# Half transposes, plain odd scores and two late sums in a sigmoid-attention and two-MLP kernel on one core

## The chip, the cores and the metric

The kernel runs on one core of a Trainium2 chip. The metric is the device time of one execution in microseconds; the figure compared is the median of several executions. The core's engines are TensorE (PE, with its weight loads shown apart as PEld), VectorE (DVE), ScalarE (ACT), GpSimd (POOL) and SyncE (SP), and 16 DMA engines move data between HBM and the core's memories.

## What is computed

Sigmoid attention over 4 batches, 12 heads, 448 positions and 64 dimensions, and then two MLP layers over the 1792 tokens it gives (768 wide, 2048 hidden). In short:

```python
scores = scale * q @ k.T - log(S)            # q, k, v: (4, 12, 448, 64) float32
attn = sigmoid(scores) @ v
x = attn moved to (1792, 768)
h = x @ w_in;  x = elu(h) @ w_out            # first layer: (1792x768)(768x2048), (1792x2048)(2048x768)
h = x @ w2_in; out = (h - tanh(h)) @ w2_out  # second layer, the same sizes
```

## The kernel before

**Numbers on PE.** PE multiplies fp32 operands in two forms. In plain fp32 one matmul is exact enough by itself. In fp32r a number is split into a head (its value copied to fp32r) and a rest (value minus head); a product is then three matmuls, head x head, head x rest and rest x head, added in PSUM. The scores and both MLP layers are made the second way, the values and the last rows of the scores in plain fp32.

**Attention** (`attention`, 16.70 to 143.80 us and its ends) works on 24 pairs of heads, two pairs to a round: an even pair n and an odd one, n + 1. Keys are taken as 384 positions in three groups of 128 (`u` = 0, 1, 2) and a rest of 64, queries as 448. The two heads of a pair lie on the two halves of the array's rows, so that the scores' matmuls come in twos. In a round PE runs, in this order: `scores` of the even pair (18 matmuls, L401); `transpose` of the next even and the next odd pair (eight and seven blocks by an identity, L332 keys, L334 the keys' rests, L336 queries); `scores` of the odd pair; `pv_rest` (L439, the rests' values); `scores_rest` (L412, the rests' scores of the next round); `pv` (L428, the values of both pairs, with the sigmoids of the even and then the odd pair). Between them, ACT and DVE drain the transposes from PSUM to `plain` (`drain`, L357 and L359) and split each pair into head and rest in `es` (`hi`, L372 and L374; `lo`, L382), and ACT makes each group of scores into weights by a sigmoid (`sig`, L422; `sig_rest`, L418). ACT and DVE also narrow the MLP weights that come in as eight-byte numbers (`load` and what it calls, L632, L635, L639), and split parts of x for the first layer (L803, L809).

**What sets the order.** Each step is an `op` with the engine's queue, a cost, the steps it waits for, and a due time from `PHASES` (with `CYCLE`, `SHIFTS`, `FIRST_PAIRS`); `Sched` simulates the engines and writes the instructions of each engine in the order that comes out. On the chip an engine runs its own list in that order and waits at each step for what the step needs. The scores, the odd transposes and the rest share three double banks of PSUM (`ring`), taken in turn; the even transposes take the values' banks (`t_flat`). A bank is free when the sigmoid, or the drain, that reads it is done.

**The MLP layers** each make their two products by a scheme of seven smaller products (P1 to P7, named in `PROD` and `W_OF`) from sums of blocks of the two operands. For the first layer's `w_out` the needed forms of the weights are made during attention, block by block: `p_sum` makes S1, S2, S3 and S4 on DVE (L692), `p_store` writes seven forms to HBM (`p_forms`) in three stores. The first layer's second product then runs from 357.3 to 560.6 us in two slices of tokens, 512 and 384 wide (`s` = 0, 1; L992), product after product; each product takes its weights in four chunks `d` of 384 KB: `ow_load` on SP's queue into one of three places in `first` (later two in `spare`), `ow_head` on ACT (L953), `ow_rest` on DVE (L957), into one of four places (places of P1, P5 and P6 are kept for the second slice). The other operand comes in half chunks `j` by `og_load`, `og_head` (L964) and `og_rest` (L968) through landing places named by the ring "g0", ten of them: seven and the temporaries 23 to 25, which lie in `second`. P3 uses S4, P7 uses S3, P6 uses S2. When a product is through, `o2_out` steps add it to the others on ACT and DVE.

## Time and profile before

| | us |
|---|---|
| median of 3 runs | 974.3 (974.08 to 976.07) |
| the profiled execution | 973.46 |
| its span in the trace | 971.7 |
| attention, up to PE's first MLP matmul | 153.94 |
| first layer's first product | 154 to 357.3 |
| first layer's second product | 357.3 to 560.6 |
| second layer | 560.6 to the end |

The span is the time between the first and the last instruction of the trace; the execution's own time holds 1.76 us more. In the timelines each row is a run of like instructions on one engine: when the first began, from there to the end of the last, engine, line, what it reads and writes, and how many. Where an engine stood idle ahead of a row, the idle time and what ended it stand in brackets at its end. PE's rows overlap, since its matmuls are pipelined: the start of a row is when the one before it has made way.

### The profile page before, as it was taken

What the parts mean: (1) busy time and instruction counts of PE and PEld (TensorE: products, weight loads), DVE (VectorE), ACT (ScalarE), POOL (GpSimd) and SP (SyncE); (2) the same over time, 40 slices, a digit from 0 to 9 for tenths busy, and PEclk for the clock granted to TensorE, in tenths of its full rate; (3) what the DMA queues carried; (4) which work ended last, traced back from release to release, by engine and by line L of the source; (5) the groups of instructions that cost most, each with busy time, mean ns of one, the idle gap of its engine ahead of it and who ended that gap; (6) DMA issues with size and microseconds to landing.
All of it is one profiled execution on the core that took longest, in us unless ns stands there. A gap on an engine that the chain in (4) does not pass through costs nothing.

```text
span 971.7 us, 15458 instructions
## 1 busy us (share of the span) xinstructions
PE 964.0 (99%) x5306; PEld 835.2 (86%) x5306; DVE 763.4 (79%) x1118; ACT 606.6 (62%) x953; POOL 101.0 (10%) x102
## 2 busy tenths in 40 slices
PE   9999999999999999999999999999999999999998
PEld 5555556889999998888999988888889999999998
DVE  4889998988888777688896988787777788666673
ACT  6889889666666675656665664444444565446652
POOL 2223311001111100000000200111111000000000
PEclk9999999999999999999999999999999999999999
DMA  8999971465555599999966416555554984545442
GB/s 250 301 348 337 331 250 38 140 224 198 188 189 181 189 303 392 412 410 398 366 223 218 139 55 244 195 191 193 187 182 169 355 288 145 145 150 180 130 145 84
DMA packets 145151, 220.18 MB, mean 227 GB/s; under 512 B 21488, under 2 KB 102960, under 8 KB 144816
## 3 DMA queue, kind: packets, MB, share of 16 engines
q1 hardware_dynamic: 143168, 218.64, 66.0%
q8 instruction: 41, 0.67, 0.3%
q10 hardware_dynamic: 1904, 0.56, 0.2%
q14 instruction: 38, 0.31, 0.1%
HBM read 143.39 MB, written 75.76 MB: 226 GB/s over the span
## 4 chain that ended last, share of the span: by engine, by line
PE 96%; DVE 1%; DMA 1%; ACT 1%; issue 0%; SPq 0%; DVEq 0%; ACTq 0%
PE psa L837 13%; PE psd L837 12%; PE psx L837 10%; PE psv L992 7%; PE psu L992 7%; PE psw L992 7%; PE psa L992 6%; PE psb L992 6%; PE psb L837 6%; PE pv L428 5%; PE sps L401 5%; PE psy L992 5%; PE psx L992 3%; PE psd L992 1%; PE pv L439 1%; PE sps L412 1%
## 5 line engine op out<-in xcount | busy, mean ns | idle before, releaser
L964 ACT ACTIVATE XB<-t 128x384 fp32r<-128x384 f32 (+1 forms) x111 | 62.0, 563 | 29.5 <-PE psw L992 8.4
L422 ACT ACTIVATE an<-sps,bias 128x896 f32<-128x896 f32 x72 | 70.5, 1020 | 12.1 <-PE sps L401 11.8
L968 DVE TENSOR_TENSOR XB<-t,XB 128x384 fp32r<-128x384 f32 (+1 forms) x111 | 68.3, 625 | 4.6 <-ACT XB L964 4.5
L752 POOL TENSOR_TENSOR second<-second 128x384 f32<-128x384 f32 x13 | 14.6, 1120 | 546.0 <-DMA spare<-p_forms 209.9
L428 PE MATMUL pv<-an,vl 128*64 128x448 f32 x288 | 56.8, 543 | 0.0
L837 PE MATMUL psa<-XB,W 128*128 128x512 f32 x192 | 54.2, 391 | 0.0
L401 PE MATMUL sps<-e 64*128 64x448 f32 x432 | 52.8, 380 | 0.6 <-ACT plain L357 0.4
L964 ACT ACTIVATE XB<-spare 128x512 fp32r<-128x512 f32 (+1 forms) x72 | 40.8, 571 | 19.0 <-DMA spare<-x_forms 5.5
L401 PEld LDWEIGHTS sps<-e 64*128 64x128 f32 x432 | 37.5, 184 | 16.7 <-issue 8.0
L428 PEld LDWEIGHTS pv<-an,vl 128*64 128x64 f32 x288 | 19.6, 137 | 36.3 <-issue 31.7
L968 DVE TENSOR_TENSOR XB<-spare,XB 128x512 fp32r<-128x512 f32 (+1 forms) x72 | 44.0, 621 | 8.4 <-ACT XB L964 8.4
L254 POOL COPY first<-raw_qk 128x384 f32<-128x384 f32 (+1 forms) x44 | 37.6, 877 | 90.2 <-DMA raw_qk<-in_k_dram 45.6
L992 PE MATMUL psu<-XB,XB 128*128 128x384 f32 (+1 forms) x192 | 46.2, 348 | 0.0
L992 PE MATMUL psv<-XB,XB 128*128 128x384 f32 (+1 forms) x192 | 46.2, 348 | 0.0
L992 PE MATMUL psw<-XB,XB 128*128 128x384 f32 (+1 forms) x192 | 46.2, 348 | 0.0
L837 PEld LDWEIGHTS psa<-XB,W 128*128 128x128 f32 x192 | 36.0, 188 | 7.5
L870 ACT ACTIVATE spare<-spare 128x512 f32<-128x512 f32 (+1 forms) x64 | 36.7, 576 | 1.4
L992 PE MATMUL psa<-XB,XB 128*128 128x384 f32 (+1 forms) x156 | 36.9, 347 | 0.0
L992 PE MATMUL psb<-XB,XB 128*128 128x384 f32 (+1 forms) x156 | 36.9, 347 | 0.0
L992 PEld LDWEIGHTS psu<-XB,XB 128*128 128x128 f32 x192 | 34.7, 188 | 1.9
L992 PEld LDWEIGHTS psv<-XB,XB 128*128 128x128 f32 x192 | 34.7, 188 | 1.9
L992 PEld LDWEIGHTS psw<-XB,XB 128*128 128x128 f32 x192 | 34.7, 188 | 1.9
(372 smaller groups left out, 2703.5 us busy)
## 6 DMA issues: line engine op xcount, KB each, us to landing
x_forms<-R1b SPq DMA_DIRECT2D x58, 256.0 KB, 2.0
first<-p_forms SPq DMA_DIRECT2D x36, 384.0 KB, 6.8
t<-x_forms SPq DMA_DIRECT2D x64, 192.0 KB, 3.1
t<-x_forms SPq DMA_DIRECT2D x47, 256.0 KB, 5.0
x_forms<-t SPq DMA_DIRECT2D x46, 256.0 KB, 2.0
x_forms<-R1b SPq DMA_DIRECT2D x58, 192.0 KB, 3.0
first<-in_moe_w_in_dram SPq DMA_DIRECT2D x13, 768.0 KB, 5.7
second<-in_moe_w_in_dram SPq DMA_DIRECT2D x13, 768.0 KB, 6.2
```

The lines of the kernel that those rows point to most:

```text
L254: nc.gpsimd.tensor_copy(out=(ql, kl)[w][:, n % NL].rearrange("p c (h d) -> p c h d", h=2), in_=x)
L401: nc.tensor.matmul(out=ps[:, j, :S], lhsT=e[lanes, EW * kz + u * 128:EW * kz + (u + 1) * 128], rhs=e[lanes, EW * qz + KW:EW * qz + EW], st ...
L412: nc.tensor.matmul(out=ps[c:c + 64, j, :S], lhsT=plain[0][lanes, RS * x:RS * x + RS], rhs=kq(x)[lanes, KW:], start=True, stop=True,)
L422: nc.scalar.activation(out=a, in_=T.pop(("s", n, u))[:, :, :S], func=ACTF.Sigmoid, bias=bias, scale=scale)
L428: nc.tensor.matmul(out=T["o", n][D * j:D * j + D, :S], lhsT=vl[m % NVL][:, x, 3 * j + u], rhs=a[:, j], start=False, stop=(u == 2), skip_gr ...
L439: nc.tensor.matmul(out=T["o", n][D * j:D * j + D, :S], lhsT=vrest[n // NR % 2][lanes, m % (NR // 2), j], rhs=a[lanes, j], start=True, stop ...
L752: by.tensor_tensor(out=out, in0=x, in1=y, op=op)
L837: nc.tensor.matmul(out=ps, lhsT=w[wz][:, k0:k0 + 128], rhs=xs[xz][:, kk], start=(opens and n == 0), stop=(n == 3 * KH - 1), skip_group_che ...
L870: nc.scalar.activation(out=r, in_=r, func=ACTF.Exp, scale=-1.0)
L964: nc.scalar.activation(out=at_place(og_place[i, s, p, j], 0, i)[:, :HW[s]], in_=T["graw", i, s, p, j], func=ACTF.Copy)
L968: nc.vector.tensor_tensor(out=lo, in0=T.pop(("graw", i, s, p, j)), in1=f(hi), op=ALU.subtract)
L992: nc.tensor.matmul(out=T["o2", tag], lhsT=lhsT, rhs=rhs, start=(p in OPENS and j == 0 and x == 0), stop=(j == NG - 1 and x == 2), skip_gro ...
```

## The change

The change has three parts, and the due times of attention (`CYCLE` 5800 for 6000, `PHASES`) are set anew with them.

1. *Transposes in halves.* From pair 4 on (`OWN`), a block of 128 x 128 is transposed as two halves, one on the upper 64 rows of the array and one on the lower 64, into two PSUM banks: 16 matmuls for the even pair, 14 for the odd one. The blocks come out 128 columns wide, so that queries are kept with 16 columns of padding to each 112 (`queries`), cleared once. The drains become two copies, one for each half of `plain`.
2. *Scores.* Only even pairs from the second on are split (`split`), head and rest both on DVE. Odd pairs and the first pair multiply in plain fp32: 6 matmuls where 18 were. There is a third tile of `plain` for it.
3. *The first layer's second product.* `p_sum` makes S1 and S2 only, and `p_forms` holds five forms. S4 = A12 - S2 and S3 = A22 - S2 are made when they are needed: `ow_load` brings A12 or A22, and once for both S2 (into `second`), and `ow_sum` subtracts on DVE. P3 and P7 run side by side: chunk 0 of P3, chunk 0 of P7, chunk 1 of P3, and so on (`o_bits`). "g0" has seven landing places.

```diff
-CYCLE = 6000
+CYCLE = 5800
+OWN = 4
@@ attention
-            krest = [ld_p.tile([128, 2, DD], F32, name=f"krest{i}") for i in range(2)]
+            krest = [first[:, NL * (R + 3) * DD + 2 * DD * i:][:, :2 * DD].rearrange("p (m x) -> p m x", m=2) for i in range(2)]
+            def split(n):
+                return n % 2 == 0 and n > 0
+            def plain_of(n):
+                return plain[1 + n // 2 % 2 if n % 2 else 0]
             def side_by_side(n, w):
+                if w == 0 and OWN <= n < OWN + NL:
+                    nc.gpsimd.memset(ql[96:, n % NL], 0.0)
             def transpose(n):
+                if n >= OWN:
+                    for i in range(len(blocks(n))):
+                        turn(n, i)
+                    return
+            def blocks(n):
+                return ([] if n % 2 else [krest[n // NR % 2][:, n // 2 % 2]]) + [kl[:, n % NL, c] for c in range(3)] + [ql[:, n % NL, c] for c in range(R)]
+            def turn(n, i):
+                ps, x = t_flat(n), blocks(n)[i]
+                for z in range(2):
+                    lanes = slice(64 * z, 64 * z + 64)
+                    nc.tensor.transpose(ps[z][:, 64 * i:64 * i + 64], x[lanes], ident[lanes, lanes])
             def drain(n, x):
+                if n >= OWN:
+                    m = len(blocks(n))
+                    out = plain_of(n).rearrange("p (i x) -> p i x", x=128)[:, :m, 64 * x:64 * x + 64]
+                    in_ = t_flat(n)[x].rearrange("p (i x) -> p i x", x=64)[:, :m]
             def hi(n):
-                if hi_on(n) == "ACT":
-                    nc.scalar.activation(out=es[n % 2][:, :EW], in_=kq(n), func=ACTF.Copy)
-                else:
-                    nc.vector.tensor_copy(out=es[n % 2][:, :EW], in_=kq(n))
+                nc.vector.tensor_copy(out=e[:, :EW], in_=kq(n)[:, :EW])
             def scores(n, u):
-                for x, (kz, qz) in enumerate(((0, 0), (0, 1), (1, 0))):
+                for x, (kz, qz) in enumerate(((0, 0), (0, 1), (1, 0)) if split(n) else ((0, 0),)):
                     for j in range(2):
                         lanes = slice(64 * j, 64 * j + 64)
+                        ks, qs = (e[lanes, EL * z:EL * z + EL] if split(n) else kq(n)[lanes, :EL] for z in (kz, qz))
                         nc.tensor.matmul(
-                            out=ps[:, j, :S], lhsT=e[lanes, EW * kz + u * 128:EW * kz + (u + 1) * 128], rhs=e[lanes, EW * qz + KW:EW * qz + EW],
+                            out=by_chunk(ps[:, j, :S]), lhsT=ks[:, u * 128:(u + 1) * 128], rhs=queries(qs[:, KW:]),
@@ weights of the first layer's second product
             def p_store(j, c):
-                part, at, a0, a1 = ((2, 0, 0, 1), (3, 0, 1, 3), (3, 2, 3, 7))[c]
+                part, at, a0, a1 = ((2, 0, 0, 1), (3, 0, 1, 3), (3, 2, 3, 5))[c]
+            def o_bits(s):
+                firsts, lasts = o_order(0, s)[:3], o_order(0, s)[5:]
+                bits = [(p, d) for p in firsts for d in range(NG // 2)]
+                bits += [(p, d) for d in range(NG // 2) for p in ("P3", "P7")]
+                return bits + [(p, d) for p in lasts for d in range(NG // 2)]
+            OF_TWO = {"P3": "A12", "P7": "A22"}
+            def ow_load(i, s, p, d, x):
+                t = ow_raw(i, s, p, d) if x == 0 else ow_other(i, s, p, d)
+                form = OF_TWO.get(p, W_OF[p]) if x == 0 else "S2"
+                nc.sync.dma_start(out=t.rearrange("p (j e) -> p j e", j=2), in_=p_forms()[:, FORMS.index(form), 2 * d:2 * d + 2])
+            def ow_other(i, s, p, d):
+                return second[:, d % 2 * CW:(d % 2 + 1) * CW]
+            def ow_sum(i, s, p, d):
+                t = ow_raw(i, s, p, d)
+                nc.vector.tensor_tensor(out=t, in0=t, in1=ow_other(i, s, p, d), op=ALU.subtract)
-                RINGS["g0"] = tuple(old) + (5, 6) + tuple(sorted((t for t in held if t not in old), key=held.get)) + (23, 24, 25)
+                RINGS["g0"] = tuple(old) + (5, 6) + tuple(sorted((t for t in held if t not in old), key=held.get))
-                for x in W_SUMS:
+                for x in ("S1", "S2"):
                     op("p_sum", (j, x), "DVE", dve(DH), p_sum, both + stored + ...)
```

How the instructions stand on the engines, before and after. A row is a line, an operation, what it writes and reads, the size, and how many of it follow each other; a number behind a name tells apart tiles that follow each other in one place.

On PE, one round in the middle of attention, before: `pv_488` and `pv_489` hold the even pair's transposes, `sps` the odd pair's and the scores; `e_83` is the even pair's split, `e_123` the odd pair's.

```order
L401 MATMUL sps<-e_83 128x448 x18
L332 MATMUL pv_488<-ident,first 128x128 x3
L334 MATMUL pv_488<-ident,krest_116 128x128
L336 MATMUL pv_489<-ident,first 128x112 x4
L332 MATMUL sps<-ident,first 128x128 x3
L336 MATMUL sps<-ident,first 128x112 x4
L401 MATMUL sps<-e_123 128x448 x18
L439 MATMUL pv_545<-ar,vrest_118 64x448 x2
L439 MATMUL pv_548<-ar,vrest_118 64x448 x2
L412 MATMUL sps<-plain_121 64x448 x2
L412 MATMUL sps<-plain_122,plain_121 64x448 x2
L428 MATMUL pv_545<-an,vl_119 64x448 x6
```

A round of the kernel after, from the last of the even pair's half transposes (L367) on; `plain_121` and `plain_119`, `plain_120` are drained pairs.

```order
L367 MATMUL pv_326<-ident,first 128x64
L367 MATMUL pv_327<-ident,first 128x64
L367 MATMUL sps<-ident,first 128x64 x14
L421 MATMUL sps<-plain_121 128x448 x6
L459 MATMUL pv_383<-ar,vrest_115 64x448 x2
L459 MATMUL pv_386<-ar,vrest_115 64x448 x2
L432 MATMUL sps<-plain_119 64x448 x2
L432 MATMUL sps<-plain_120,plain_119 64x448 x2
L448 MATMUL pv_383<-an,vl_118 64x448 x6
L448 MATMUL pv_386<-an,vl_118 64x448 x6
L421 MATMUL sps<-e_83 128x448 x18
```

The order of the steps is the same; the odd pair's 18 matmuls on `e_123` have become 6 on `plain_121`, behind 14 half transposes.

On ACT, one round of attention before: from the three sigmoids of an even pair (L422) to those of the next.

```order
L422 ACTIVATE an<-sps,bias 128x896 x3
L357 ACTIVATE plain_121<-pv_625 128x512
L357 ACTIVATE plain_122<-sps 128x832
L422 ACTIVATE an<-sps,bias 128x896
L632 ACTIVATE XB_71<-XB_71 128x768
L422 ACTIVATE an<-sps,bias 128x896
L372 ACTIVATE e_83<-plain_121 128x832
L418 ACTIVATE ar<-sps,bias 128x896
L422 ACTIVATE an<-sps,bias 128x896
L632 ACTIVATE R1b<-R1a 128x768
L803 ACTIVATE XA<-R0a 128x512
```

The same on ACT after (L442 the sigmoids, L388 the drains, L651 the narrowing, L822 the copies of parts of x).

```order
L442 ACTIVATE an<-sps,bias 128x896 x3
L388 ACTIVATE plain_121<-sps 128x7x64
L388 ACTIVATE plain_119<-pv_738 128x8x64
L442 ACTIVATE an<-sps,bias 128x896
L651 ACTIVATE XB_71<-XB_71 128x768
L651 ACTIVATE XB_71<-XA_70 128x768
L442 ACTIVATE an<-sps,bias 128x896 x2
L438 ACTIVATE ar<-sps,bias 128x896
L822 ACTIVATE XA<-R0a 128x512
L651 ACTIVATE R1b<-R1a 128x768
```

The odd pair's drain has moved ahead of the even pair's, the split's copy (L372) is gone, and the two narrowing steps stand side by side behind the first sigmoid of the odd pair.

On DVE, at P3's first weights in the wide slice, before: rests of weights (L957), each behind its head on ACT, among rests of the other operand (L968) and narrowing of the second layer's weights (L635, L639).

```order
L957 TENSOR_TENSOR XB_72<-first,XB_72 128x768
L968 TENSOR_TENSOR XB_1753<-t,XB_1753 128x512
L635 TENSOR_SCALAR R1b<-R1b 128x768
L639 SCALAR_TENSOR_TENSOR R1b<-R1b 128x768
L968 TENSOR_TENSOR XB_1753<-spare,XB_1753 128x512
L957 TENSOR_TENSOR XB_72<-first,XB_72 128x768
L968 TENSOR_TENSOR XB_1753<-t,XB_1753 128x512
L635 TENSOR_SCALAR R1a<-R1a 128x768
L639 SCALAR_TENSOR_TENSOR R1a<-R1a 128x768
L968 TENSOR_TENSOR XB_1753<-t,XB_1753 128x512
L957 TENSOR_TENSOR e_83<-first,e_83 128x768
```

The same place after (L993 the rests of weights, L986 the new sums, L1004 the other operand's rests, L654 and L658 the narrowing).

```order
L986 TENSOR_TENSOR first<-first,second 128x768
L1004 TENSOR_TENSOR XB_1711<-t,XB_1711 128x512
L658 SCALAR_TENSOR_TENSOR R1a<-R1a 128x768
L1004 TENSOR_TENSOR XB_1711<-t,XB_1711 128x512
L654 TENSOR_SCALAR R1b<-R1b 128x768
L993 TENSOR_TENSOR XB_72<-first,XB_72 128x768
L1004 TENSOR_TENSOR XB_1711<-spare,XB_1711 128x512
L658 SCALAR_TENSOR_TENSOR R1b<-R1b 128x768
L986 TENSOR_TENSOR first<-first,second 128x768
L1004 TENSOR_TENSOR XB_1711<-spare,XB_1711 128x512
L986 TENSOR_TENSOR first<-first,second 128x768
L993 TENSOR_TENSOR XB_72<-first,XB_72 128x768
```

A sum stands ahead of each rest, several steps before it, and two of the sums follow each other with one step between.

## Rows read from the trace of the kernel before

**Rows 1.** Part 1 of the page: busy time, share of the span, instructions, by engine.

```profile
PE 964.0 (99%) x5306; PEld 835.2 (86%) x5306; DVE 763.4 (79%) x1118; ACT 606.6 (62%) x953; POOL 101.0 (10%) x102
```

**Rows 2.** Table of stretches: length, busy by engine, granted clock, DMA share, GB/s.

```profile
16.70:143.80 127.10, 126.72 (x938) 69.95 (x934) 112.57 (x166) 109.18 (x135) 33.29 (x38) 1.00 0.98 318
407.90:440.50 32.60, 32.60 (x145) 27.02 (x144) 26.11 (x38) 20.91 (x33) 0.00 (x0) 1.00 1.04 412
```

**Rows 3.** PE's timeline of one round: start, us, instruction, count, idle before and releaser.

```profile
95.24 2.09 PE L401 MATMUL sps<-e 64*128 64x448 f32 x18
97.26 0.55 PE L332 MATMUL pv<-ident,first 128*128 128x128 f32 x3
...
97.75 0.55 PE L336 MATMUL pv<-ident,first 112*128 112x112 f32 x4
98.14 0.49 PE L332 MATMUL sps<-ident,first 128*128 128x128 f32 x3
98.47 0.55 PE L336 MATMUL sps<-ident,first 112*128 112x112 f32 x4
98.94 2.18 PE L401 MATMUL sps<-e 64*128 64x448 f32 x18
101.06 0.98 PE L439 MATMUL pv<-ar,vrest 64*64 64x448 f32 x8
101.86 0.54 PE L412 MATMUL sps<-plain 64*64 64x448 f32 x1
...
102.72 4.73 PE L428 MATMUL pv<-an,vl 128*64 128x448 f32 x24
107.38 0.47 PE L401 MATMUL sps<-e 64*128 64x448 f32 x2
```

**Rows 4.** ACT's timeline of the same round.

```profile
96.15 2.81 ACT L422 ACTIVATE an<-sps,bias 128x896 f32<-128x896 f32 x3 [0.24 <-PE sps L401]
```

**Rows 5.** Groups by line in attention: count, busy, mean ns, idle before.

```profile
L401 PE MATMUL sps<-e 64*128 64x448 f32 x396 | 47.9, 380 | 0.4 <-ACT plain L357 0.4
```

**Rows 6.** Weight loads of the transposes, in the timeline of PE's loading side.

```profile
97.26 0.20 PEld L332 LDWEIGHTS pv<-ident,first 128*128 128x128 f32 x2 [0.30 <-issue]
```

**Rows 7.** ACT's timeline of round 2, the round that stalls.

```profile
34.45 0.90 ACT L632 ACTIVATE R1b<-R1a 128x768 f32<-128x768 f32 x1 [2.11 <-DMA R1a<-in_moe_w_in_dram]
35.26 2.78 ACT L422 ACTIVATE an<-sps,bias 128x896 f32<-128x896 f32 x3
...
38.41 0.88 ACT L357 ACTIVATE plain<-sps 128x832 f32<-128x832 f32 x1
```

**Rows 8.** PE's timeline of round 2.

```profile
39.34 0.87 PE L401 MATMUL sps<-e 64*128 64x448 f32 x6 [0.37 <-ACT plain L357]
...
41.80 0.60 PE L428 MATMUL pv<-an,vl 128*64 128x448 f32 x2
```

**Rows 9.** PE's timeline at the start: the first scores.

```profile
7.61 2.72 PE L401 MATMUL sps<-e 64*128 64x448 f32 x18
```

**Rows 10.** ACT's timeline of a round whose operand comes late.

```profile
71.34 0.64 ACT L803 ACTIVATE XA<-R0a 128x512 fp32r<-128x512 f32 x1 [1.23 <-DVE R0a L450]
```

**Rows 11.** PE's timeline of the last round: both pairs' scores in a row.

```profile
143.80 4.64 PE L401 MATMUL sps<-e 64*128 64x448 f32 x36
```

**Rows 12.** ACT's timeline of the narrow slice (P3, then P7): heads of weights.

```profile
520.04 0.85 ACT L953 ACTIVATE e<-first 128x768 fp32r<-128x768 f32 x1 [0.86 <-PE psb L992]
...
523.16 0.85 ACT L953 ACTIVATE W<-first 128x768 fp32r<-128x768 f32 x1 [0.86 <-PE psb L992]
```

**Rows 13.** DVE's timeline of the wide slice: rest of P7's third chunk.

```profile
423.47 0.95 DVE L957 TENSOR_TENSOR e<-first,e 128x768 fp32r<-128x768 f32 x1
```

**Rows 14.** DVE's timeline of the narrow slice: rest of the chunk headed at 523.16.

```profile
524.04 0.96 DVE L957 TENSOR_TENSOR W<-first,W 128x768 fp32r<-128x768 f32 x1 [0.22 <-ACT W L953]
```

**Rows 15.** DMA issues: count, KB each, us from issue to landing.

```profile
first<-p_forms SPq DMA_DIRECT2D x36, 384.0 KB, 6.8
```

More of the change, by code (lines that the diff above doesn't have):

```diff
@@ L279, in when @@
             def when(kind, n, *rest):
-                at, first = PHASES[kind], FIRST_PAIRS.get((n, kind), 0)
+                if (n, kind) in FIRST_PAIRS:
+                    return FIRST_PAIRS[n, kind]
+                at = PHASES[kind]
                 if kind not in ("sr", "sigr", "pvr", "ldk", "ldv", "ldqk1"):
@@ L285, in when @@
                     at = at[rest[0]]
-                return n * ROUND + at + first + (0 if kind in ("s", "sig", "pv") else SHIFTS.get((n, kind), 0))
+                return n * ROUND + at + (0 if kind in ("s", "sig", "pv") else SHIFTS.get((n, kind), 0))
             def loads(m):
@@ L354, in drain @@
                 else:
[L355 removed]
+                    out, in_ = queries(kq(n)[:, KW:]), by_chunk(t_flat(n)[1][:, :S])
                 if by == "ACT":
@@ L412, in scores_rest @@
                         nc.tensor.matmul(
-                            out=ps[c:c + 64, j, :S], lhsT=plain[0][lanes, RS * x:RS * x + RS], rhs=kq(x)[lanes, KW:], start=True, stop=True,
+                            out=by_chunk(ps[c:c + 64, j, :S]), lhsT=plain[0][lanes, RS * x:RS * x + RS], rhs=queries(kq(2 * m + x)[lanes, KW:KW + R * 128]), start=True, stop=True,
                         )
@@ L1034, in mlp @@
             last = NPR - 1
-            before_early = [("lo", last), ("sr", NPR // 2 - 1)] + [("s", last, u) for u in range(3)] + [("sig", last, u) for u in range(3)]
+            before_early = [("lo", last - 1), ("sr", NPR // 2 - 1)] + [("s", last, u) for u in range(3)] + [("sig", last, u) for u in range(3)]
             before_late = [("xdone", last)]
@@ L1394, in first_out @@
                 scratch_free[0] = list(stage_frees[0])
-                stage_frees[1] = [d for t in (23, 24, 25) for d in turn_of[f"t{t}"]]
+                stage_frees[1] = [d for n in range(2) for d in raw_free["second", n]]
                 sp0, sp1 = raw_free["spare", 0], raw_free["spare", 1]
```

149 lines of the change are left out of this document (75 added, 74 removed).

## The prediction, made before the changed kernel was run

> **What bounds the kernel now.** First the totals of the page: TensorE (PE) is busy in 964.0 of 971.7 us [rows 1], so an edit pays only where it takes time from PE's own row of instructions, or adds a wait to it. Then the table of stretches, for the stages the diff touches: attention runs to 153.94 us, the first layer's second product from 358 to 561; the granted clock is 1.00 in all of them (its higher level, 2.4 GHz) [rows 2]. Attention also keeps the DMA engines (0.98), VectorE (DVE, 112.57 of 127.10) and ScalarE (ACT, 109.18) nearly full [rows 2]. Third, PE's own timeline of one round of attention (two pairs of heads): scores of the even pair 95.24, its successors' transposes 97.26 and 98.14, scores of the odd pair 98.94, rest of the values 101.06, rest of the scores 101.86, values 102.72, next round 107.38 [rows 3]. That is 12.14 us with no idle time marked. Last ACT's timeline of the same round [rows 4], since it empties the banks that PE fills: its three sigmoids of the even pair start at 96.15, 0.91 after the scores, and end at 98.96.
>
> **The change in attention, part by part.** *Transposes.* Now eight blocks take 97.26 to 98.14 and seven 98.14 to 98.94, together 1.68 us, 0.11 each. The last four of the odd pair take 0.47 where the same four of the even pair take 0.39 (98.47 to 98.94, 97.75 to 98.14) [rows 3]: the 0.08 is the change of tiling before the scores. The change makes each block two halves of 64 columns on two halves of the array, in the tiling that the scores have. A half moves half the columns, so 0.055; the scores show that two such halves do run together (18 matmuls in 2.02 us, of which each lasts 0.38 by its group) [rows 3, 5], and a weight load of a transpose does not hold them up: two of them, 0.14 each, take 0.20 together, so the second starts 0.06 after the first [rows 6]. If the halves pair up, 15 x 0.055 = 0.83; if not, 30 x 0.055 = 1.65. I take 0.87, near the lower end because these two rows are the nearest, and the even scores lose their 0.08 at the end: 2.02 becomes 1.94.
>
> *Odd scores in plain fp32.* Three fp32r products of 9 pairs of matmuls become one fp32 product of 3 pairs. The nearest rows are plain fp32 matmuls of the same 448 columns. The rest of the scores, which run side by side as one, take 0.86 (101.86 to 102.72), some 0.1 of it a change of tiling; the values, 24 records in six pairs, 102.72 to 107.38, 0.78 a pair with two such changes [rows 3]. Without them 0.75 a pair. Three pairs: 2.24, plus 0.05 for the first and 0.1 for the change of tiling behind: 2.39 against 2.12 now (98.94 to 101.06). If ACT and DVE were always ready, a round would go from 12.14 to 12.14 - 0.81 - 0.08 + 0.27 = 11.52.
>
> *What is late next.* They are not ready. Three double banks go round: even scores 1, 2, 3, odd transposes, odd scores 1, 2, 3, rest. So odd scores 1 wait for the even pair's second sigmoid, odd scores 2 for its third, odd scores 3 for the drains of the odd transposes. Neither the sigmoids nor what starts them moves. Walk the round from 95.24: even scores to 97.18, transposes to 98.05; second sigmoid ends near 98.06 (96.15 + 0.90 + 1.01), odd scores 1 start 98.12; third ends 98.96 [rows 4], odd scores 2 start 99.02 (a release takes 0.05: 38.41 + 0.88 to 39.34 [rows 7, 8]) and, after a standstill, take 0.80, to 99.82; odd scores 3 to 100.57, plus 0.1; then 0.80, 0.86 and 4.66 as now. The odd drain stands directly behind the third sigmoid on ACT and its half of about 0.55 us ends by 99.45, before it is asked for. Next round at 106.99 instead of 107.38: **0.39 us less a round**, 0.23 short of 11.52. It also says that the transposes' size matters little: up to 98.16, 1.0 us, nothing moves.
>
> *Which rounds.* Ten rounds (107.38 is one of them) get new transposes; the first four pairs keep the old. Start: the first scores, 18 matmuls from 7.61, take 2.7 with waits for drains [rows 9]; with no split they start some 0.1 earlier and take 2.4, 0.3 less; the second pair's 2.1 becomes 2.4 as above: together -0.1 at the first values, 16.70. Round 1: -0.39. Round 2 has the one long stall: ACT waits 2.11 us for a load of weights, and its sigmoids stand behind that, 35.26 to 38.04, the third group of the odd scores at 39.34 after a wait, values at 41.80 [rows 7, 8]. In the change's order this narrowing still stands ahead of those sigmoids, and its load still stands behind the same loads on SP's queue, so I keep 35.26: odd scores 2 at 38.10, values at 41.41. The gain up to there is then 0.39 in all and what was won before is lost. Eight more rounds: 8 x 0.39 = 3.12. One of them has its sigmoids late, behind an operand that waits for a DVE step of the values' drain: its scores start near 16.70 + 4 x 12.14 + 0.8 + 4.66 = 70.7, the sigmoid is due 0.91 later, at 71.6, and the operand's copy, from 71.34, lasts 0.64 [rows 10], so some 0.2 late; DVE has less to do, I count half, 0.1. Last round: both scores, 36 matmuls in a row from 143.80, take 4.6, paced by the sigmoids [rows 11]; with three fp32 pairs behind the same sigmoids +0.1. Sum: -0.39 - 3.12 - 0.1 + 0.1 = **-3.5 us** (bounds: -4.9 if the round-2 load comes in time, since 10 x 0.39 + 0.8 + 0.2; about +0.6 if halves don't pair, below).
>
> *What is hidden.* The odd pairs' splits leave DVE, the even split's first half moves from ACT to DVE, and two of four sums leave each of eight weight blocks. All of this lies beside PE, and only keeps it covered. The third store of each block shrinks from four forms to two, 8 x 384 KB = 3.1 MB less of 127.10 us x 318 GB/s = 40 MB [rows 2], so DMA should keep pace with a round 3% shorter. Two clears on GpSimd stand ahead of query copies; it is busy 33.29 of the 127.10 [rows 2], so I count nothing.
>
> **The change in the second product.** PE's matmuls are the same in number and size, only P3 and P7 now alternate by weight chunk (32.60 / 8 = 4.08 us each in the wide slice [rows 2]; 3.12 in the narrow one, 520.04 to 523.16 [rows 12]). Added per slice: four loads of 384 KB and eight sums of a 128x768 block on DVE, 0.96 each by the rest's row [rows 13, 14], 7.7 us. Cover: in the wide slice the worst weights are ready at 423.47 + 0.95 = 424.42 for P7's third chunk, used two chunks into it, at 407.90 + 6 x 4.08 = 432.4: 8.0 us of lead [rows 2, 13]. In the narrow slice a head starts at 523.16, the moment its place (one of four) is free, and its rest ends at 525.00; use is three chunks after 523.16, so 7.5 us of lead [rows 12, 14]. Cost of the cover: DMA share is 1.04 in the wide slice [rows 2], so 4 x 0.39 MB at 412 GB/s puts 3.8 us on what follows; DVE is busy 26.11 in the 32.6 us of P3 and P7 [rows 2], with 7.7 that is 33.8, 1.2 over. 5.0 of lag against 8.0 of lead: I count **0**; if the cover is gone, the lag beyond 8.0 falls on PE one to one. P7 also opens one chunk after P6 instead of four, 4.08 or 3.12 us in which ACT, 20.91 busy of the 32.60 [rows 2], must copy three tiles of a scheme's sums: enough. The rest of the kernel is untouched.
>
> **Sum.** The profiled execution took 973.46, 1.76 more than its span; -3.5 gives 970.0. The runs' median is 974.3, so 0.84 above it: **970.8 us**. 0.2%, about what can be told from no change here, is 1.95 us.
>
> **The rivals.** *(a) The halves don't pair.* Then 15 x 0.109 = 1.64 stands where 1.68 was, odd scores start 98.82 without a wait and end, with 2.39, at 101.21: +0.15 a round. Nine rounds +1.3, with round 2 still -0.39 and the ends 0: 974.3 + 0.9 = 975.2, within 0.2%. For it: nothing of that form is in the trace. Against it: the scores' pairs in the same tiling. The Trainium skill speaks for it (TensorE: Matmul & The Clock Gate, LDWEIGHTS): a weight load takes its columns at 1.2 GHz whatever its rows; a half has the same 128 columns as a whole block, so by an estimate from that page 0.107 a pair, and the time of this rival. The trace is against so high a price for a transpose's load: the second starts 0.06 after the first [rows 6]. *(b) ACT late.* PE now waits directly for the third sigmoid, so whatever stands ahead of the first one costs one to one. Round 2 shows 0.8 of it (41.80 against 16.70 + 2 x 12.14 = 40.98), the round at 71.34 some 0.2 [rows 3, 8, 10]; if most rounds get 0.2, nine times 0.2 gives back 1.8: 972.6. *(c) More gain,* round 2's load in time: -4.9, 969.4. *(d) Slower: the weights of P3 and P7 come late.* The landing places of the other operand fall from ten to seven, 3 x 2.04 = 6.1 us less ahead; with the 5.0 above 11.1 of lag, 3.1 beyond the lead, for 973.9. It decides once the lag passes 8.0 + 3.5 = 11.5; to be slower by 0.2% it needs 13.4, one load more behind a blocked SP queue (6.8 from issue to landing [rows 15]), which gives 11.1 + 6.8 - 8.0 - 3.5 = +6.4: 980.7. Against it: the lead stays near 8 in all of P7, P2 and P4 though DMA is full.
>
> **How the numbers follow.** Forecast 0.56, (a) 0.10, (b) 0.15, (c) 0.09, (d) 0.10, of which half ends between -0.4 and no verdict and half slower. Faster: forecast and (c), 0.65, and the milder part of (b): 0.69. Slower: half of (d) and the late end of (a): 0.09. Same: 0.22. The range 968.6 to 975.2 takes in (a), (b), (c) and the bounds of the forecast (970.8 with 0.15 a round either way is 969.3 to 972.3), and leaves out the worse half of (d) and what lies below (c).
>
> **What would show it.** Right: a steady round near 11.75 us; transposes of two pairs near 0.9; odd scores with a wait on ACT's sigmoid before their second group, near 2.5 in all; values at 41.4 in round 2; the first product starting about 150.4 instead of 153.94; no idle PE between there and the second layer beyond what is there now. Wrong: transposes near 1.6 (a), a first sigmoid over 1.0 after its scores in many rounds (b), values of round 2 by 40.3 (c), PE idle before P7, P2 or P4 of the first layer (d).

## The result and the profile after

| | before | after |
|---|---|---|
| median (7 runs each) | 974.3 us (973.83 to 976.07) | 981.6 us (977.12 to 988.82) |
| the profiled execution, its span | 973.46, 971.7 | 978.59, 976.9 |

The ratio is 1.0076, with a 95% interval of 1.0049 to 1.0102: slower, where 970.8 and faster was forecast. 981.6 lies outside the range of 968.6 to 975.2. The bytes that DMA moves are the same; the page of the changed kernel shows that 3.15 MB have gone from writing to reading (before: 143.39 read, 75.76 written).

```profile
PE 966.5 (99%) x5378; PEld 826.6 (85%) x5378; DVE 760.6 (78%) x1113; ACT 597.2 (61%) x942; POOL 99.6 (10%) x105
...
HBM read 146.54 MB, written 72.61 MB: 224 GB/s over the span
```

Where the 5.3 us of the profiled execution went can be counted, since both kernels run the same 4200 matmuls in the MLP layers. The start of the first one, before and after: 153.94 and 153.07, so -0.87 from attention. The one that opens P2 in the wide slice: 440.55 and 441.20, +0.66. The one that opens P6 in the narrow slice: 498.17 and 501.38, +3.21. Fifteen matmuls behind it: 500.77 and 505.62, +4.84. The last: 967.39 and 972.66, +5.27. So attention gained 0.9, the stretches up to the two openings of products lost 1.5 and 2.6, the fifteen matmuls behind the second lost 1.6, and the rest 0.4.

PE's timeline of the changed kernel at the two openings, where 1.18 and 2.27 us of this stand as idle time:

```profile
439.18 0.84 PE L1028 MATMUL psw<-XB,W 128*128 128x512 f32 x3
441.20 0.94 PE L1028 MATMUL psy<-XB,XB 128*128 128x512 f32 x3 [1.18 <-DVE R0a L1042]
...
498.43 0.69 PE L1028 MATMUL psw<-XB,XA 128*128 128x384 f32 x3
501.38 0.81 PE L1028 MATMUL psu<-XB,XB 128*128 128x384 f32 x3 [2.27 <-ACT R1a L1046]
502.02 0.91 PE L1028 MATMUL psv<-XB,XB 128*128 128x384 f32 x3
502.74 1.16 PE L1028 MATMUL psw<-XB,XB 128*128 128x384 f32 x3
```

PE waits neither for weights nor for the other operand. It waits for the copy (`o2_out`) that takes the last product out of the PSUM banks which the new product is to use. Behind the second pause three matmuls last 1.16 where they lasted 0.68. The table of stretches shows why: the granted clock is 0.86 there, and the trace has it at the lower level from 502.32 to 505.73. That part is no fixed price of a stall: in the second profile of this kernel, below, P6 stalls for 2.77 and the clock stays at 1.00. The stretches of the kernel before come first (columns: length, PE, PEld, DVE, ACT, POOL busy, clock, DMA share, GB/s), then those of the changed one:

```profile
473.00:485.50 12.50, 12.50 (x73) 12.46 (x72) 9.86 (x15) 7.87 (x13) 0.00 (x0) 1.00 0.98 343
485.50:498.00 12.50, 12.50 (x74) 12.50 (x73) 11.44 (x16) 8.50 (x15) 0.00 (x0) 1.00 0.91 312
498.00:510.50 12.50, 12.50 (x74) 12.50 (x74) 11.55 (x15) 9.15 (x17) 0.00 (x0) 1.00 0.46 142
```

```profile
473.00:485.50 12.50, 12.50 (x72) 12.30 (x72) 11.35 (x19) 8.13 (x15) 0.00 (x0) 1.00 1.01 363
485.50:498.00 12.50, 12.50 (x74) 12.50 (x73) 11.40 (x16) 6.80 (x12) 0.00 (x0) 1.00 1.02 381
498.00:510.50 12.50, 10.23 (x50) 9.91 (x49) 10.86 (x15) 8.84 (x16) 0.00 (x0) 0.86 0.64 216
```

DMA's share was 0.98, 0.91 and 0.46 in these stretches; it is 1.01, 1.02 and 0.64 now. Over the whole of 360 to 498 us the share was 1.01 and is 1.02, and DMA moved 383 GB/s and moves 390: about 1 MB more, where 3.15 MB more are asked for, so that other transfers move back. All eight extra loads of S2 are issued ahead of 498 us, as the tile `second` shows in the changed kernel (ns shortest, median and longest of an issue, then the starts of the first and the last):

```profile
L979 SPq DMA_DIRECT2D second<-p_forms x8: 319/320/400, 376.4 to 483.5; - x8
```

The opening itself, on ACT before and then after (L1010 and L1046 are the copies; P6 opened at 498.17 before):

```profile
495.64 0.92 ACT L964 ACTIVATE XB<-second 128x384 fp32r<-128x384 f32 x2
496.81 0.53 ACT L964 ACTIVATE XB<-t 128x384 fp32r<-128x384 f32 x1 [0.25 <-PE psw L992]
497.33 0.49 ACT L1010 ACTIVATE R1a<-psu 128x384 f32<-128x384 f32 x1
```

```profile
499.66 0.89 ACT L651 ACTIVATE R1b<-R1b 128x768 f32<-128x768 f32 x1
500.45 0.51 ACT L1000 ACTIVATE XB<-t 128x384 fp32r<-128x384 f32 x1
500.86 0.46 ACT L1046 ACTIVATE R1a<-psu 128x384 f32<-128x384 f32 x1
```

Before, the copy ended at 497.82, 0.35 us ahead of P6: the tightest place of the stage, since P1, which P6 follows at once in this slice, uses the same banks. Now P1 ends near 498.95 and ACT comes to the copy at 500.86. From 496.05 on ACT works without a gap; what made it late stands ahead of that, first on ACT and then on DVE:

```profile
491.75 0.53 ACT L1000 ACTIVATE XB<-spare 128x384 fp32r<-128x384 f32 x1 [1.64 <-DMA spare<-x_forms]
493.18 0.53 ACT L1000 ACTIVATE XB<-spare 128x384 fp32r<-128x384 f32 x1 [0.91 <-DMA spare<-x_forms]
496.05 1.50 ACT L822 ACTIVATE XB<-R0a 128x1536 fp32r<-128x1536 f32 x1 [1.85 <-DVE R0a L812]
```

```profile
492.93 0.95 DVE L986 TENSOR_TENSOR first<-first,second 128x768 f32<-128x768 f32 x1
493.80 0.55 DVE L1004 TENSOR_TENSOR XB<-spare,XB 128x384 fp32r<-128x384 f32 x1
494.27 1.75 DVE L812 TENSOR_TENSOR R0a<-R0a 128x1536 f32<-128x1536 f32 x1
```

ACT stands before two operands that land late, and then before a DVE step (L812), which stands in DVE's list behind a new sum (L986) and behind the rest of the second of these operands (L1004). The opening of P2 in the wide slice has a chain of the same kind: there ACT stood 2.78 us, up to 435.98, before a store of narrowed weights (`w_forms`), DVE then 2.05 before what ACT narrows, and DVE's copy came at 440.38.

PE's timeline of a round in the middle of attention, against [rows 3]:

```profile
94.69 2.11 PE L421 MATMUL sps<-e 64*128 64x448 f32 x18
96.64 0.66 PE L367 MATMUL pv<-ident,first 64*128 64x64 f32 x16
97.13 0.60 PE L367 MATMUL sps<-ident,first 64*128 64x64 f32 x14
97.64 2.67 PE L421 MATMUL sps<-plain 64*128 64x448 f32 x12
100.24 0.98 PE L459 MATMUL pv<-ar,vrest 64*64 64x448 f32 x8
...
106.57 0.68 PE L421 MATMUL sps<-e 64*128 64x448 f32 x4
```

A round lasts 11.88 instead of 12.14: even scores 1.95, transposes 1.00 (1.68 before), odd scores 2.60 (2.12 before). The start is another matter. Four blocks of queries take 0.75 there (6.37 to 7.12), where the same four of the kernel before took 0.40 (6.25 to 6.65):

```profile
6.37 0.95 PE L357 MATMUL pv<-ident,first 112*128 112x112 f32 x4
7.12 0.85 PE L353 MATMUL sps<-ident,first 128*128 128x128 f32 x3
...
8.64 3.58 PE L421 MATMUL sps<-plain 64*128 64x448 f32 x12
```

PE ran at half its pace until about 11 us, and the first values began at 18.87 instead of 16.70.

### The profile page after: what moved, and what is told of

Read it like the earlier page. It is cut to its first block, busy times and chain, and to the rows that moved or that the text cites. A ratio compares the mean times of both kernels' runs of the same rounds, so it can differ in the third digit from the quotient of the medians.

```text
span 976.9 us, 15659 instructions
## 1 busy us (share of the span) xinstructions
PE 966.5 (99%) x5378; PEld 826.6 (85%) x5378; DVE 760.6 (78%) x1113; ACT 597.2 (61%) x942; POOL 99.6 (10%) x105
## 4 chain that ended last, share of the span: by engine, by line
PE 80%; DMA 16%; DVE 2%; ACT 1%; issue 1%; SPq 0%; ACTq 0%; DVEq 0%
PE psa L856 13%; PE psd L856 11%; PE psx L856 9%; PE psb L856 6%; PE pv L448 5%; PE sps L421 5%; PE psu L1028 4%; PE psv L1028 4%; PE psw L1028 4%; DMA first<-p_forms 4%; PE psb L1028 4%; PE psa L1028 4%; PE psx L1028 3%; PE psy L1028 3%; DMA t<-x_forms 2%; DMA w_forms<-R1b 2%
## 5 line engine op out<-in xcount | busy, mean ns | idle before, releaser
L1000 ACT ACTIVATE XB<-t 128x384 fp32r<-128x384 f32 (+1 forms) x125 | 69.3, 562 | 28.2 <-PE psw L1028 6.8
L1004 DVE TENSOR_TENSOR XB<-t,XB 128x384 fp32r<-128x384 f32 (+1 forms) x125 | 76.8, 624 | 5.9 <-ACT XB L1000 5.9
L442 ACT ACTIVATE an<-sps,bias 128x896 f32<-128x896 f32 x72 | 69.8, 1011 | 18.9 <-PE sps L421 12.2
L1000 ACT ACTIVATE XB<-spare 128x512 fp32r<-128x512 f32 (+1 forms) x83 | 47.1, 572 | 26.8 <-DMA spare<-x_forms 12.2
L1004 DVE TENSOR_TENSOR XB<-spare,XB 128x512 fp32r<-128x512 f32 (+1 forms) x83 | 50.9, 621 | 9.7 <-ACT XB L1000 9.5
L448 PEld LDWEIGHTS pv<-an,vl 128*64 128x64 f32 x288 | 19.6, 137 | 36.3 <-issue 34.4
L270 POOL COPY first<-raw_qk 128x384 f32<-128x384 f32 (+1 forms) x44 | 35.1, 806 | 86.9 <-DMA raw_qk<-in_k_dram 46.4
L421 PE MATMUL sps<-plain 64*128 64x448 f32 x156 | 36.1, 587 | 0.1
L856 PE MATMUL psa<-XA,e 128*128 128x512 f32 x144 | 36.0, 394 | 0.0
```

Of the source, the lines that this page charges most:

```text
L270: nc.gpsimd.tensor_copy(out=(ql, kl)[w][rows, n % NL].rearrange("p c (h d) -> p c h d", h=2), in_=x)
L421: nc.tensor.matmul(out=by_chunk(ps[:, j, :S]), lhsT=ks[:, u * 128:(u + 1) * 128], rhs=queries(qs[:, KW:]), start=(x == 0), stop=(x == 2 or ...
L442: nc.scalar.activation(out=a, in_=T.pop(("s", n, u))[:, :, :S], func=ACTF.Sigmoid, bias=bias, scale=scale)
L448: nc.tensor.matmul(out=T["o", n][D * j:D * j + D, :S], lhsT=vl[m % NVL][:, x, 3 * j + u], rhs=a[:, j], start=False, stop=(u == 2), skip_gr ...
L856: nc.tensor.matmul(out=ps, lhsT=w[wz][:, k0:k0 + 128], rhs=xs[xz][:, kk], start=(opens and n == 0), stop=(n == 3 * KH - 1), skip_group_che ...
L1000: nc.scalar.activation(out=at_place(og_place[i, s, p, j], 0, i)[:, :HW[s]], in_=T["graw", i, s, p, j], func=ACTF.Copy)
```

## The experiments

The first theory was that the side-by-side order is to blame: P2 opens one chunk after P3's end instead of four. Four kernels took the change apart. *Attention alone* leaves the second product as before; *second product alone* is the rest of the diff; the third has only the order of `o_bits`, with S3 and S4 still made in attention; the fourth has the sums without that order and reads S2 for P3 and for P7 anew:

```diff
-                bits += [(p, d) for d in range(NG // 2) for p in ("P3", "P7")]
+                bits += [(p, d) for p in ("P3", "P7") for d in range(NG // 2)]
...
-                                if p == "P3":
-                                    op("ow_load", (0, s, p, d, 1), ...)
+                                op("ow_load", (0, s, p, d, 1), ...)
```

**Attention alone.**

> The kernel before with the attention part of the change alone (half transposes, plain odd scores, its due times); the four sums stay in attention and the second product is that of before. Theory (the loss sits in the second product, where PE waits for banks at the opening of products): no PE idle over 0.3 us between 357 and 561 beyond that of before, and 971.2 us if the start runs as in the kernel before (16.7 to the first values), 973.4 us if the start is as late as in the trace after (18.87). Rival (attention's new order of ACT and DVE is what delays the second product): the stalls of 1.3 and 2.4 us stay, 976 to 978 us.

977.0 us, ratio 1.0034 (1.0018 to 1.0050). The second product doesn't stall, as the theory has it, but attention does: its first MLP matmul starts at 156.50, later than before. The rounds are 11.87 up to 65 us, but for round 2, and up to 13.4 behind that. PE's timeline shows what it waits for:

```profile
87.04 0.46 PE L367 MATMUL sps<-ident,first 64*128 64x64 f32 x8 [0.88 <-POOL first L270]
```

That is a copy of queries and keys on GpSimd, which waits for its load. With four forms still in the third store of each block, seven in all, DMA (share 0.98 to 1.00) can't feed the shorter rounds.

**Second product alone.**

> The kernel before with the second-product part alone (two sums made there, P3 and P7 side by side, seven landing places); attention is that of before. Theory: the stalls of the trace after are there again, 1.3 us at P2 of the wide slice and 2.4 us at P7 of the narrow one with some 1.6 us at the lower clock behind: 974.3 + 5.3 = 979.6 us, with runs that spread by several us. Rival (attention's order causes them): 974.3 us within 1.

979.2, ratio 1.0056 (1.0034 to 1.0079). The stalls are there: 0.75 at P7 and 1.54 at P2 of the wide slice, 3.05 at P6 of the narrow one (the expectations up to the eleventh run name it P7; it is P6 that opens there).

**The order alone.**

> The kernel before, only with P3 and P7 of the first layer's second product side by side by weight chunk; all four sums stay in attention, ten landing places stay, no sums on DVE in the second product. Theory (a product opens one chunk after the product whose banks it takes has ended, and the copies that empty them stand late in ACT's and DVE's lists): PE idle at P2 of the wide slice and at P7 of the narrow one, 1 to 2.5 us each, 977 to 980 us. Rival (the sums on DVE and their loads make everything late): no such stalls, 974.3 us within 1.

973.6, ratio 0.9990 (0.9980 to 1.0001), and no idle PE between 405 and 510 us. The theory falls here.

**The sums without the order.**

> The second-product part without the side-by-side order: P3 is made whole, then P7, each with its own loads of S2 (four more of 384 KB a slice than the change) and its sums on DVE; seven landing places. Theory (the order is the cause, not the sums): no new PE stall at the opening of a product, 974.3 us within 1. Rival (the sums and loads are the cause): stalls of 1 us and more in P3, P7 or P2, 977 to 981 us.

991.9, ratio 1.0172 (1.0146 to 1.0199): the slowest of the four, with sixteen extra loads instead of eight. P6 of the narrow slice waits longest here:

```profile
511.93 1.33 PE L1009 MATMUL psu<-XB,XB 128*128 128x384 f32 x3 [7.22 <-ACT R1a L1027]
```

So the sums or their loads cost the time. The next four tell these apart.

**No loads, no sums.**

> The changed kernel without what it adds to the second product: no extra loads of S2 and no sums there; P3 takes S2 and P7 takes S1 as their weights, so S3 and S4 are computed nowhere (that part of the computation is left out). Attention is that of the change, P3 and P7 stay side by side, seven landing places. Theory (extra loads and sums are what costs time in the second product, and attention is shorter by 3 us when two sums have left it): no PE stall over 0.3 us in the second product; 974.3 - 3.0 = 971.3 us if the start is as in the kernel before, 973.5 us if it is 2.2 us late as in the trace of the change. Rival (seven landing places or the order cause the stalls): 976 us and more.

974.2 (971.22 to 976.33), ratio 0.9993 (0.9982 to 1.0005). The profile, of the fastest execution, has no stall in the second product and its first MLP matmul at 151.25, 2.7 earlier than before. Seven landing places instead of ten do no harm.

**The loads, with hardly any sum.** To the run with the order alone:

```diff
+            def ow_sum(i, s, p, d):
+                t = second[:, d % 2 * CW:d % 2 * CW + 8]
+                nc.vector.tensor_tensor(out=t, in0=ow_raw(i, s, p, d)[:, :8], in1=t, op=ALU.subtract)
```

> The kernel of the side-by-side run (all sums in attention) with the change's four extra loads of S2 a slice and its seven landing places, but instead of each sum a DVE step of only 8 columns whose result nobody uses. Theory A (the loads: DMA is full there, so what lands behind them lands late): stalls at P2 of the wide and P7 of the narrow slice, 976 to 979 us. Theory B (the sums' 0.95 us each on a DVE that is nearly full): no stall over 0.3 us, 973.6 us within 1.

983.3, ratio 1.0088 (1.0068 to 1.0108): 9.7 us more than the order alone, for eight loads. DVE is busy only 9.74 and 11.26 of 12.5 us ahead of P6's opening. ACT's timeline shows the chain:

```profile
503.77 0.52 ACT L978 ACTIVATE XB<-t 128x384 fp32r<-128x384 f32 x1 [3.09 <-DMA t<-x_forms]
504.20 0.87 ACT L632 ACTIVATE R1b<-R1b 128x768 f32<-128x768 f32 x1
504.97 0.92 ACT L978 ACTIVATE XB<-t 128x384 fp32r<-128x384 f32 x2
505.80 0.48 ACT L1024 ACTIVATE R1a<-psu 128x384 f32<-128x384 f32 x1
```

ACT stands 3.09 us before an operand that has not landed. That operand is not needed for several microseconds yet (PE uses it at 515.29), but the copies that P6 needs now are behind it in ACT's list. Here the chain has no sum in it. Of the 9.7 us, PE idles 0.99, 0.72 and 3.56 at P7, P2 and P6; a stretch at the lower clock behind P6 (505.19 to 512.01 in this profile) is in them too.

**The loads, with sums of full size.**

> As the run with the extra loads and 8-column steps, with the DVE steps at their full 768 columns (0.95 us each; the result is still unused, the stored S3 and S4 are multiplied). Theory A (loads): about the time of that run. Theory B (DVE): 3 to 5 us longer than that run, 977 to 980 us, with ACT's copies of P6's and P3's banks late.

984.8 (980.40 to 988.14), ratio 1.0112 (1.0083 to 1.0142). The intervals of this and the run before overlap: the sums' time on DVE adds nothing that four runs can tell, though in the profile they stand in the chain, as in the changed kernel (ACT waits 1.87 for the same DVE step).

**The sums on GpSimd.**

> The changed kernel with its sums in the second product on GpSimd, which has no work between 357 and 561 us, instead of DVE. Theory B (DVE full): the stalls of 1.3 and 2.4 us shrink below 0.5 us, 971 to 974 us. Theory A (loads), or a sum on GpSimd that lasts over 2 us and so makes the weights late: the stalls stay, 977 us and more.

986.1, ratio 1.0109 (1.0091 to 1.0128). A sum takes 2.26 us there, and PE now also waits for operands (2.37 at 483.71). It stalls for 3.47 at P6 all the same.

Three kernels then asked whether an order can save it: copies first in the lists, the same bytes with P3 and P7 in a row, and heads planned later.

```diff
+                def emptied(s, p, d):
+                    at = {("P3", 1): "P6", ("P2", 1): "P3"}.get((p, d))
+                    return [("o2_out", 0, s, at, t) for t in o2_tiles(0, s)] if at else []
```

> The changed kernel with another order alone: heads and rests of the weights and operands for P3's second chunk stand behind the copies that empty P6's banks in ACT's and DVE's lists, those for P2's second chunk behind P3's. Theory C (the loads lag by some 3 us, ACT and DVE stand waiting for a landing, and the copies behind that landing come late for a product that opens one chunk after the other's end): the stalls at P2 of the wide and P7 of the narrow slice fall below 0.5 us each, 972 to 975 us by the start. Rival (whatever the order, the lag of the loads comes out on PE): stalls of 2 us and more in all, 977 us and more.

985.3, ratio 1.0116 (1.0089 to 1.0143), stalls of 2.31 and 4.07 us. (In this kernel the sum of P3's second chunk can take a later chunk of S2, so a part of P3 is not the product's.)

> The kernel before (sums in attention, P3 whole and then P7) with the same four extra loads of 384 KB a slice as the change, spread evenly over P3 and P7, each used by a DVE step of 8 columns only, and seven landing places: the load of DMA of the run with extra loads, without the side-by-side order. Theory C: a product opens four chunks after the banks' last use, so that late copies do no harm: operands' leads shrink by some 3 us and PE stalls stay below 0.5 us, 974 to 975.5 us. Rival (the loads alone cost what they cost, in any order): stalls of 3 us and more, 979 to 983 us.

985.2, ratio 1.0112 (1.0088 to 1.0136). The wide slice has no stall here, so the side-by-side order does make its openings tight. But the narrow slice loses 6.5 us at two places:

```profile
496.53 0.62 PE L1006 MATMUL psu<-XB,XA 128*128 128x384 f32 x2 [3.48 <-DVE XB L982]
...
507.50 0.86 PE L1006 MATMUL psu<-XB,XB 128*128 128x384 f32 x3 [3.04 <-ACT R1a L1024]
```

> The changed kernel with the planner's estimate of a load's landing in the second product raised from 5.0 to 9.0 us (weights and the other operand), which moves heads and rests further back in ACT's and DVE's lists and changes nothing else. Theory C: the copies of banks stand ahead of what has not landed, stalls at openings shrink to under 1 us in all, 972 to 975 us; if operands then come late instead, PE waits at chunks rather than at openings. Rival: stalls as in the changed kernel, 978 us and more.

991.0, ratio 1.0186 (1.0152 to 1.0219). P6's opening no longer stalls, and other places do (2.27 at P7 of the wide slice, 4.19 at P4 of the narrow one, 560.60, there for weights). None of the three orders gave the time back. The price of eight loads isn't one number, though: 979.2 with the second product alone, 981.6 in the changed kernel (with the new attention), 983.3 with hardly any sum, 985.2 in a row. Each kernel gets other lists of the engines, and how much of a stall is the loads' lag and how much the place that a list gives to a copy isn't told apart by these runs.

What was left is the bytes. Two kernels test it. The first holds back six of the narrow slice's early loads until PE is well into P1; in its trace all twelve loads of P3 and P7 in that slice, four of them of S2, are issued from 494.95 on, where the changed kernel issued those four from 415.93 to 483.54. The second has half the extra loads.

```diff
+                            if s == 1 and p in OF_TWO and d < 2:
+                                stored = stored + [("o2", 0, 1, "P1", 5, 0)]
```

> The changed kernel with the narrow slice's loads for the first two chunks of P3 and P7 (A12, A22 and S2, six of 384 KB) put behind the sixth eighth of that slice's P1 in SP's list, about 12 us later than now and out of the stretch in which DMA is full (share 1.02 up to 498 us, 0.64 behind it). Theory D (the bytes that DMA has to move up to 498 us decide when P1's copies come, which have 0.35 us of margin at P6's opening in the narrow slice): the stall of 2.4 us and the 1.6 us of lower clock behind it go, the 1.4 us at P2 of the wide slice stays: 972 to 975 us by the start. Rival (sums and copies on DVE and ACT keep P6's opening late in any case): the stall stays, 977 us and more.

977.7, ratio 1.0038 (1.0024 to 1.0051). The stall at P6 is gone, DMA's share is 0.94 and 0.88 up to 498 us and 0.98 behind it. The wide slice still loses 0.73 and 0.22, and the second layer now waits 1.59 for weights at 619 us, so that its time lies between those of the two kernels.

> The run with extra loads of S2 and 8-column DVE steps, but the extra loads in the wide slice alone: four of 384 KB instead of eight. Theory D (lag adds up over both slices, 0.95 us a load, against a margin that is used up near eight): the stall at P6 of the narrow slice shrinks from 3.7 us to 1 us or less; 975 to 978 us. Rival (each slice's loads harm that slice alone): P6's stall in the narrow slice goes altogether, what the wide slice lost (2 us) stays, 976 us.

976.8, ratio 1.0033 (1.0014 to 1.0052). Four loads in the wide slice alone leave that slice without a stall and stall P6 in the narrow one:

```profile
500.30 0.79 PE L1006 MATMUL psu<-XB,XB 128*128 128x384 f32 x3 [1.11 <-ACT R1a L1024]
```

ACT had stood 2.01 us before an operand that stands ahead of the copies in its list:

```profile
497.71 0.53 ACT L978 ACTIVATE XB<-t 128x384 fp32r<-128x384 f32 x1 [2.01 <-PE psw L1006]
```

The profile puts this wait down to PE, whose group ends at 497.64; the operand's own load landed at 497.61, so either can have ended it. DMA's share is 1.05 from 473 to 498, against 1.02 and 0.79 in its two halves with the order alone. So a load in one slice is paid for in the next. By extra loads, with nothing else but the landing places and 8-column steps: none 973.6, four 976.8, eight 983.3. P6 waits 0, 1.11 and 3.56 us in them.

> The run without extra loads and sums once more (S3 and S4 are left out as there), for a second profile of the same program: its ten times spread from 971.2 to 976.3 us though the second product does not stall. If the spread is made at the start (TensorE at its lower clock up to about 12 us in some executions), the first values start at 17.0 or at 18.9 us and all else is alike; if it is made in the rounds (queries and keys that land late on a full DMA), rounds of 12.2 us and more stand between rounds of 11.87.

972.7 in a second execution with a quick start (values at 16.89). Its first MLP matmul is at 151.75, but it waits 1.17 us at 200.53 in the first product, where the first profile of this program waits 0.18 and the kernel before not at all. Six of the nine profiles with the new attention have a wait there, 0.18 to 1.17, and none of the eight with the old; it doesn't go by the time at which PE comes out of attention, and its cause is not shown.

> The changed kernel once more, for a second profile: whether the late start (first values at 18.87 us) comes again, and whether P6's opening in the narrow slice and P2's in the wide one stall again. Theory D: the stalls at both are there in every execution, 1 us and more each; the start is 17.0 or 18.9.

979.6. The late start is there again (18.60), and so are the stalls: 0.34 at P7, 1.66 at P2, 2.77 at P6. Over all 17 profiles the start is at half pace in nine, with the new attention (4 of 9) as with the old (5 of 8). So it is not the change's doing, though the first values then begin at 18.3 to 18.9 with the new attention and, but for one at 19.6, at 17.6 to 17.9 with the old.

## Why the prediction was wrong, point by point

**Transposes.** Right in kind, a little short: 30 halves take 1.00, not 0.87. Eight pairs in 0.49 (96.64 to 97.13) are 0.061 a pair, so they do run together and rival (a) is out. The weight loads of these transposes follow each other as closely:

```profile
96.44 0.72 PEld L367 LDWEIGHTS pv<-ident,first 64*128 64x128 f32 x16
```

What the prediction took for this from [rows 6] was thin: only the first two loads there start 0.06 apart. Of four whole-block loads of the kernel before, the later ones follow 0.10 to 0.11 apart:

```profile
97.64 0.44 PEld L336 LDWEIGHTS pv<-ident,first 112*128 112x128 f32 x4
```

So that row did not speak against the price of (a); the scores' pairs did, and with those alone to go by, the outcome was in part luck. The rate of 0.107 a pair that the estimate from the Trainium skill gave (TensorE: Matmul & The Clock Gate, LDWEIGHTS) is not what these loads show.

**Odd scores and the wait for the sigmoid.** Right: ACT's third sigmoid of the even pair ends at 98.48 in that round, the second group of odd scores starts at 98.54, and the three take 2.60 against the 2.55 of the walk. ACT, then the group's weight loads:

```profile
95.68 2.80 ACT L442 ACTIVATE an<-sps,bias 128x896 f32<-128x896 f32 x3 [0.29 <-PE sps L421]
98.54 0.30 PEld L421 LDWEIGHTS sps<-plain 64*128 64x128 f32 x4 [0.60 <-ACT an L442]
```

The round comes to 11.88 and not 11.75: the transposes' 0.06 over what the wait hid, and 0.05 in the scores. Rival (b) did not come: the first sigmoid starts 0.98 to 1.00 after its scores (0.91 before), not over 1.0. From the scores of round 3 (46.46, then 47.21) to those of the last round (143.80, 142.76), eight rounds gave 1.8 us where 3.2 was forecast: 0.13 short in each, and two of 12.27 and 12.05 in which the third group of odd scores waits for a drain.

**Round 2 and the start.** The stall of round 2 is absent in the changed kernel's profile (values 11.87 after those of the round before): its start was 2.2 us late, and the load landed meanwhile. The start was put at -0.1; it was +2.17, by a pace of TensorE that no row of the trace of before shows and that comes and goes. With a quick start attention's part was worth 2.7 and 2.2 us, 3.5 expected, and round 2 lasts 12.15 and 12.26 there, not 11.87: the whole of (c) came only with the late start. The term of the start was mis-sized by up to 2.3.

**What is hidden in attention.** Right in the changed kernel's profile, and needed: without the 3.1 MB less to store, the shorter rounds starve (attention alone, 156.50). The cover is thin. In three other profiles with the same attention PE still waits for one of GpSimd's copies behind a late load, for 0.36 to 1.13 us.

**The second product: the step that failed.** "5.0 of lag against 8.0 of lead: I count 0." The sum was made for the wrong place, and both its terms were off. First, the lag was counted by slice, four loads, 3.8 us. But all eight are issued between 376.4 and 483.5 us, those of the narrow slice far ahead of use, and DMA has no room before 498: eight loads are 3.15 MB by 412 GB/s = 7.6 us. Second, the leads held: the weights of P4's first chunk in the wide slice, to take one, are ready at 453.16 in the changed kernel, and P4 opens at 457.64: 4.5 us, less than 8.0 and still enough. What had no lead was the copy that opens P6 in the narrow slice, 0.35 us, which [rows 12] and [rows 13] don't show, since they are of weights. It stands in ACT's list behind operands that are loaded early, and these landed late. PE stood 2.27 us at it and 1.18 at P2's; no weights were late there. Counted over runs, the second product took back 7.4 us by the medians (974.2 without the loads and sums, 981.6 with them), where 0 was counted. The Trainium skill says that ACT and DVE take their instructions strictly in order (TensorE: Matmul & The Clock Gate, Architectural detail); the 3.09 us in front of the copies in the run with loads alone is that, seen. Third, "4.08 or 3.12 us: enough" for P7 was not enough either (0.26 to 1.15 us in six of the profiles with extra loads, 2.27 in one), and P2's opening behind P3, one chunk as well, was not looked at.

**The rivals.** (d) was the nearest, with a chance of 0.10: loads late in a full DMA, slower by more than 0.2%. Its place (weights) was wrong, and its landing places cost nothing. The time follows the number of extra loads (none, four and eight, above; sixteen 991.9), and about half of the 7.4 us is gone when those of the narrow slice are issued behind 494 us (977.7). That these bytes decide, and not the lists that each kernel gets with them, is the likelier reading, and not shown apart.

**What stays open.** How much of a quick start's 2 to 3 us in attention an average execution keeps: with the second product light, ten runs had a median of 974.2, the same as before. No kernel tried beat the one before beyond its interval; the order alone is the nearest at 973.6. Open too: why TensorE reaches its quick pace at such different moments, and whether another list with the same eight loads would be as fast as one without.

## What to carry to other kernels

Before moving a transfer out of one stage, find the last moment up to which DMA is full in the stage that takes it in, and add all that is moved up to there, over prefetches too: on the full queue here the lag added up and was paid at the tightest place. That place was not an operand with microseconds of lead. Look also for the copy that empties a bank for the next product, and read what stands ahead of it in its engine's list. On an engine that works its list in order, an early wait for a far operand becomes a late step for a near one (3.09 us on ACT above).

## What the hardware showed unexpectedly

TensorE ran at half its pace at first (four blocks in 0.75 instead of 0.38 to 0.47), in nine of 17 profiles up to 9.6 to 13.7 us. A trace's clock records begin with the rise to the higher level (2.4 GHz): at 5.03 us in the kernel before and 10.80 in the changed one; at 4.2 to 6.1 in the eight quick starts and at 9.6 to 13.7 in the nine slow ones. The table of stretches gives 1.00 for 6.37 to 8.64 us only because a stretch without a record counts as 1.00 there. What sets the moment of the rise is not shown. Weight loads of transposes on 64 rows keep up with pairs 0.061 us apart.
